# A row sum made with the residual, so that the MLP's centring need not wait for its statistics, and a newly searched order

## The chip, the cores and the metric

One core of a Trainium2 chip runs the whole kernel. The metric is the device time of one execution in microseconds (us); lower is better.

## The reference, cut to what matters

Two layers, each an attention block and an MLP block, on 2048 rows of 512 columns in bf16:

```python
x = x + attention(layernorm(x))       # linear attention, 32 heads, then @ wo
x = x + mlp(layernorm(x))             # relu(gate) * up, then @ W_down
x = x + attention(layernorm(x))
x = x + mlp(layernorm(x))
# layernorm(x) = (x - mean(x)) / sqrt(var(x) + 1e-5), no weights
```

The MLP is homogeneous: a factor on its input comes out squared, as relu(gate) and up both carry it. The kernel feeds it x - mean and multiplies the output by 1/(var + eps).

## The kernel before

The 2048 rows are 16 tiles of 128. Every piece of work is an operation with a cost, a rank ("due") and the buffers it takes. A planner inside the kernel turns them into one emission order; each engine runs its instructions in that order. The ranks (DUE) and the choice of ACT or DVE for copies (PLACE) are tables that a search found beforehand. The hand-over from attention to MLP of tile t:

```python
# attend(l, t, ...)
a = op("PE", mm(4, 512), ..., proj)                       # o @ wo into PSUM
a = op("DVE", dve(512), ..., lambda: nc.vector.tensor_tensor(
    out=x, in0=x, in1=yp.t[:], op=Alu.add), [a], (), [yp], name="resA")
...
# mlp(l, t0, n, ...)
for i in range(n):
    t = t0 + i
    a = stats(l, "B", t, due_x(i), [after[t]])            # bn_stats, bn_aggr -> mean, var
    seen.append(a)
    xc = Buf(p_xn)
    a = op("DVE", CENTRE, due_x(i), lambda t=t, xc=xc: nc.vector.tensor_scalar(
        out=xc.t[:], in0=x_of(t), scalar1=mv[:, t, 0:1], scalar2=None, op0=Alu.subtract), [a], [xc], name="xc", port=2)
    turned.append(turn(xc, ...))                          # transpose; tiles 0 and 1 of a layer on PE, others by DMA
r = op("DVE", ..., tmp = var + EPS, seen); r = op("DVE", ..., rs = 1 / tmp)   # shortened; used by the MLP's residual
...   # gate and up matmuls, relu, product, down matmuls, residual with rs
```

The blocks of the MLP have 1, 1, 2, 4, 4, 2, ... tiles. Only the first one or two must get through attention before PE can start on the MLP at all. For those two hand-overs, one in each layer, the chain "residual, statistics, aggregate, centring, turn, copy" is short of other work.

The softmax here doesn't subtract the row's maximum and nothing guards it: scores larger than these inputs give would overflow.

Of the kernel before, what the change touches and what calls it, by code (L numbers as in the profile page):

```python
# [8 lines left out]
P = 128  # L9
D = 512  # L10
# [26 lines left out]
class Op:  # L37
# [3 lines left out]
    def __init__(self, eng, cost, due, emit, deps=(), takes=(), uses=(), name="", move=0, port=False,  # L41
                 follow=(), alt=None):
        self.eng, (self.occ, self.lat) = eng, cost
        self.due, self.emit, self.name, self.move, self.port = due, emit, name, move, int(port)
        self.deps = [d for d in deps if d is not None]
        self.follow = [d for d in follow if d is not None]
        self.takes, self.uses = list(takes), list(uses)
        self.then, self.behind, self.alt, self.twin = [], [], alt, None
# [162 lines left out]
DVE0 = (85, 170)  # L211
RLN, REXP = ((150, 265), (203, 318)), ((145, 262), (198, 315))
# [13 lines left out]
class K:  # L226
# [9 lines left out]
    "0000000100000001001000000000100000000000010001111000011000011001110000000000011010000001001111001100"  # L236
    "0100000110110100010000011011100101111100101001111000111010100001001101101100100110011001110011001001"
    "1111001110100000000011100010100100000101001110100111000101101010101000101010111001010111100010110100"
    "0"
)  # L240
PHI = dict(POOL=("POOL", "POOL"), DVE=("DVE", "DVE"), BOTH=("DVE", "POOL"))
PHI0 = ["POOL", "POOL", "DVE"] * 5 + ["BOTH"]
PAIRN, PAIRK = 4, T
# [5 lines left out]
    76719491, 69466873, 69464194, 55720479, 42085309, 40348612, 33593703, 42085031, 50665322, 33594228, 56086954,  # L249
    58486545, 100334641, 61163217, 49431745, 41251988, 69056115, 9741064, 80414090, 80414120, 53308772, 80413780,  # L250
    106435297, 49852457, 80414139, 49848882, 56526831, 56526817, 69547873, 53741705, 49852168, 66481170, 68934086,
    55660918, 50246487, 32405931, 57594884, 55662420, 50058741, 44536605, 58281570, 3, 22509044, 49850622, 49848858,
    69548291, 69463783, 49850611, 55051722, 76716792, 0, 55324383, 47430106, 32690380, 59187722, 60929485, 45084743,
    53725584, 55713647, 55727277, 54655971, 49923445, 50246438, 55324400, 55324343, 35442704, 55802924, 35441651,
    55161101, 53685522, 51682019, 33202876, 47809082, 52941970, 53687226, 55701298, 55711066, 55655645, 44505335,
    54950229, 47610086, 55322999, 47811927, 35002194, 55588705, 62960580, 55157588, 53726567, 47768162, 55269518,
    47767416, 55571188, 53304664, 55688755, 55180830, 55625721, 50380932, 40642846, 40645264, 47809620, 55323699,
    57680173, 55268245, 54520833, 53558741, 55098763, 55683455, 55732950, 55683459, 55697315, 55770465, 52825634,
    55713412, 55710946, 55506275, 54950156, 35001190, 54949680, 34999890, 59085355, 62960363, 54948116, 55748897,
    55646532, 56083290, 53268545, 59116845, 55619542, 55763775, 53310977, 55774953, 55764998, 55740543, 52826475,  # L260
    55685321, 52784010, 55711099, 55519531, 56373630, 50382939, 52826205, 52825598, 55778163, 55771090, 55181433,
    55768958, 55684488, 55709355, 55684978, 55522442, 55648291, 55646610, 55689548, 54948629, 55098862, 47766546,
    54948487, 56010726, 55697946, 55693442, 55936025, 53268542, 44506128, 55691384, 55769572, 55545075, 55409199,
    55692897, 55662797, 55667892, 55709660, 55713749, 55700261, 55690361, 55371927, 55946741, 55947245, 55372043,
    55396376, 55760995, 55660101, 55570763, 55708913, 55708943, 50191721, 55658940, 55569634, 55658937, 55655528,
    52824974, 54566163, 55181604, 56093099, 55623488, 55927755, 55388217, 55697886, 55645404, 55667208, 55921043,
    55691484, 55685094, 55623151, 55652318, 55396329, 55703531, 55760168, 55699699, 55388529, 55623507, 55651900,
    55396324, 56045911, 55709610, 55623568, 55048436, 55709159, 56660851, 55240452, 55696214, 55974927, 55693988,
    55741153, 55693228, 55396401, 55665438, 55487833, 55388179, 55703473, 55388150, 55305368, 57292002, 55522439,
    55570606, 54081536, 55694997, 57095763, 45526601, 45175404, 54082167, 55710694, 56661198, 55697150, 54522450,  # L270
    47668141, 45175447, 49709693, 50191138, 48930643, 51185210, 41476757, 41476428, 56663182, 55710691, 55700162,
    55966393, 55623154, 55694078, 55418211, 55667889, 55662695, 50622534, 54522884, 55759099, 54522768, 55305365,
    53814510, 54207260, 51926549, 56731158, 22533505, 86923532, 49054124, 54577294, 50454445, 56663443, 26743223,
    64933030, 26742771, 41476589, 77848357, 55701636, 46564931, 86922882, 76909815, 56851302, 56665549, 49600025,
    49129654, 50619771, 50620709, 50622827, 56301309, 54209613, 56114277, 54821759, 49333488, 51487502, 52263956,
    39762113, 19221682, 41476432, 41476507, 40958443, 51486441, 50279390, 16984712, 37300570, 50960427, 49597502,
    35848215, 39760598, 24648533, 41476504, 55699989, 55704953, 48137801, 50278843, 46562185, 37300567, 49597307,
    49597499, 35844120, 55705982, 39761347, 49335617, 38759704, 49337568, 39761346, 55750849, 56154495, 33592791,
    56153063, 32405860, 51221336, 55803472, 55693594, 55803225, 55321390, 55802697, 53688156, 49597175, 49597541,
    49597913, 49596963, 58672801, 49543902, 49597043, 49596659, 55778023, 55771093, 55123240, 55776845, 55771414,  # L280
    55772175, 53557771, 53310277, 53304643, 44505573, 53310550, 55124938, 56045945, 55661057, 55711116, 55624256,
    55667825, 55396537, 56736587, 57094903, 54082104, 57408271, 54209459, 57094884, 55827685, 46563699, 56440267,
    55828521, 55702687, 46562936, 55705068, 48140907, 48140902, 56553271, 55701218, 55705063, 55720810, 56440270,
    48141651, 55702429, 55696714, 55697995, 59129153, 55703718, 55704014, 55827014, 48137480, 46562610, 30585230,
    58655341, 49560287, 21530914, 52917937, 47182136, 30584484, 55701037, 46563696, 52917833, 41444195, 41443940,
    47181589, 47181495, 41443844, 55700488, 53497782, 38496984, 56130655, 55690360, 55704606, 53137802, 55693769,
    55703325, 53137820, 55692042, 50947124, 55405040, 50987789, 41443966, 41414378, 55870566, 52917866, 55300343,
    55700485, 52129878, 61996903, 62505784, 55697736, 53137801, 55550154, 55700626, 55740601, 55699572, 55699299,
    55704914, 55699024, 58344346, 62506293, 50451565, 49470778, 53245447, 53278134, 49336219, 55704076, 55886670,
    55697360, 53497785, 55550159, 55699902, 55700360, 55698793, 55698582, 52841760, 55869605, 55108122, 54090734,  # L290
    55300268, 62506063, 62660753, 62506806, 55705573, 49344780, 55886105, 55700933, 49470866, 56146496, 55700624,
    55692773, 55692770, 55701615, 55740476, 49312541, 55752952, 49765942, 55886212, 55430767, 55238713, 55977103,
    55691820, 55688056, 47612654, 55699803, 55700555, 55697628, 55700835, 55741749, 55700975, 55702709, 55575076,
    55692884, 53991858, 53991972, 53990466, 54779534, 53853809, 54779664, 55691422, 55704463, 55620232, 55701498,
    55691964, 55738452, 55702685, 56001882, 55694740, 55702008, 55709199, 55691466, 55067255, 54761274, 56123195,
    55807312, 53991318, 53863952, 53762021, 55604349, 55704395, 55702362, 55614451, 55885531, 55702411, 55692752,
    55709972, 55702819, 56002178, 55480865, 55231139, 54147794, 57042018, 52613586, 55611316, 55693850, 55704710,
    55704869, 55540072, 55704035, 55707614, 55708907, 55702786, 55415742, 55707642, 55704187, 55610312, 55706936,
# [146 lines left out]
def kernel(  # L445
# [328 lines left out]
    def attend(l, t, due, eq, made, how):  # L774
# [4 lines left out]
        for k in range(3):  # L779
# [36 lines left out]
            for b in range(NB)], [a] + l_wo, [yp], [oT], name="proj")  # L816
        x = x_of(t)
        a = op("DVE", dve(512), due + 3, lambda: nc.vector.tensor_tensor(out=x, in0=x, in1=yp.t[:], op=Alu.add), [a],  # L818
               (), [yp], name="resA")
        return pe, a  # L820


# [207 lines left out]
```

## Time and profile before

| | before |
|---|---|
| time, median of 6 runs | 386.45 us (385.96 to 386.70) |
| span of the profiled run | 384.4 us |
| PE busy, DVE, ACT | 375.9, 316.6, 211.1 us |
| matmuls, of which fillers (warm-up included) | 2834, 15 |

In the views, one line is a group of instructions: start, length, engine, source line, operation, output<-inputs, shapes, count; in brackets the engine's idle time just before and who ended it. PE is the matmul engine, PEld its weight loads. Of the names, xn is a centred tile and xnTB its turned (transposed) form, o is the attention's output and oT the same turned, N holds copied numerators of the attention. Fillers are matmuls on zeros, whose result nobody reads.

Busy PE hides refills, and the trace of the changed kernel lacks the records of 45 of its matmuls, so busy and idle sums of these two traces cannot be compared (a later trace of it has all 2832; see the end). I use an **account of lost PE time** instead. All 2832 or 2834 weight loads are in the traces, one per matmul, in program order. Each matmul is given its streaming time, columns/2.4 + 2.5 ns; the traces show that rate in unbroken streams (4 matmuls of 512 columns 0.86 us, 16 of 128 columns 0.89 us). Fillers (matmuls on zeros, whose result nobody reads) count nothing. The work is then 365.98 us. What the clock shows at a weight load, less the work done by then, is the time lost so far. The work mark (12 us of work, 48 us of work, ...) is the same point of progress only roughly, since orders differ, and weight loads start ahead of their matmul (in before by 0.05 to 0.21 us in a stream, by up to 0.74 where the matmul waits). So differences below 0.2 us between marks say little.

### The profile page before, as it was taken

To read this page: it belongs to the slowest core of one execution; us is meant where nothing else is said; L and a number is where in the kernel's file an instruction comes from. 1 tells how busy PE (TensorE), PEld (TensorE's weight loads), DVE (VectorE), ACT (ScalarE), POOL (GpSimd) and SP (SyncE) were. 2 spreads that over 40 slices of the span, in tenths; PEclk is the share of its full clock that TensorE was granted. 3 is DMA by queue.
4 is the path that set the end of the run, shared out by engine and by line. 5 is a ranking of instruction groups with operands and counts; after the bars stand their busy time and mean duration, and the time that the engine had idled before them with its cause. 6 is when DMAs were issued, how large, how long until landed. Compare 5 with 4: busy or idle time off the path is not lost.

```text
span 384.4 us, 7669 instructions
## 1 busy us (share of the span) xinstructions
PE 375.9 (98%) x2834; PEld 226.1 (59%) x2834; DVE 316.6 (82%) x804; ACT 211.1 (55%) x545; POOL 40.6 (11%) x43
## 2 busy tenths in 40 slices
PE   8999998999999999999999999999999999999996
PEld 5454555877654445445666654587765445446775
DVE  6999999999999999586686688999999795565442
ACT  5999999634557215573274479955444513421431
POOL 0256720000002100050031021000000000000000
PEclk9999999999999999999999999999999999999999
DMA  8398730133222224201110000012333313002110
GB/s 226 78 232 219 176 118 2 38 69 63 41 57 55 44 41 57 55 2 34 29 35 2 15 15 1 2 32 47 79 67 81 72 23 88 0 14 77 32 31 29
DMA packets 60869, 22.83 MB, mean 59 GB/s; under 512 B 52672, under 2 KB 59808, under 8 KB 60832
## 3 DMA queue, kind: packets, MB, share of 16 engines
q1 hardware_dynamic: 60416, 21.95, 25.3%
q10 hardware_dynamic: 416, 0.39, 0.4%
q8 instruction: 22, 0.36, 0.4%
q14 instruction: 15, 0.12, 0.1%
HBM read 7.91 MB, written 2.10 MB: 26 GB/s over the span
## 4 chain that ended last, share of the span: by engine, by line
PE 84%; DVE 12%; issue 2%; ACT 1%; DVEq 0%
PE b L878 33%; PE b L911 17%; PE b L676 7%; PE b L682 7%; PE b L814 5%; PE b L764 5%; PE q L782 3%; PE b L854 3%; PE q L723 2%; DVE bstB L637 1%; DVE hT L886 1%; PE q L584 1%; DVE bstA L637 1%; DVE pr L807 1%; DVE gu L591 1%
## 5 line engine op out<-in xcount | busy, mean ns | idle before, releaser
L878 PE MATMUL b<-xnTB,wgu 128*128 128x128 bf16 (+2 forms) x1200 | 151.8, 279 | 0.3 <-ACT xnTB L590 0.3
L878 PEld LDWEIGHTS <-wgu 128*128 128x128 bf16 x1200 | 98.0, 98 | 44.1 <-issue 0.4
L911 PE MATMUL b<-wd,hT 128*128 128x512 bf16 (+2 forms) x363 | 85.9, 373 | 0.0
L882 ACT ACTIVATE gu<-b 128x512 bf16<-128x512 f32 (+1 forms) x83 | 48.4, 584 | 57.9 <-PE b L878 54.3
L706 POOL TENSOR_TENSOR phiK<-ek,sk 128x512 bf16<-128x512 bf16 x37 | 39.9, 1101 | 193.2 <-ACT sk L697 190.7
L886 DVE TENSOR_TENSOR hT<-gu 128x512 bf16<-128x512 bf16 (+1 forms) x83 | 34.8, 420 | 24.2 <-ACT gu L590 22.9
L911 PEld LDWEIGHTS <-hT 128*128 128x128 bf16 (+1 forms) x363 | 34.0, 98 | 30.8 <-DVE hT L886 0.3
L679 ACT ACTIVATE ek<-b 128x512 bf16<-128x512 f32 x64 | 35.4, 604 | 16.6 <-PE b L676 16.5
L687 DVE TENSOR_REDUCE sk<-ek 128x64 f32<-128x1024 bf16 x32 | 38.5, 1211 | 3.4 <-ACT ek L679 3.2
L768 ACT ACTIVATE Eq<-b 128x512 bf16<-128x512 f32 x64 | 36.1, 623 | 1.6 <-PE b L764 1.4
L814 PE MATMUL b<-wo,oT 128*128 128x512 bf16 x128 | 32.9, 379 | 0.5 <-ACT oT L590 0.5
L918 DVE SCALAR_TENSOR_TENSOR X<-b,rsB,X 128x512 bf16<-128x512 f32 (+1 forms) x33 | 23.6, 724 | 11.8 <-PE b L911 11.6
L590 ACT CAST gu<-b 128x512 bf16<-128x512 f32 (+1 forms) x42 | 24.4, 581 | 16.2 <-PE b L878 16.1
L590 ACT CAST N<-q 128x384 bf16<-128x384 f32 (+1 forms) x60 | 26.9, 464 | 11.3 <-PE q L782 8.5
L682 PE MATMUL b<-wv,xnTA 128*128 128x512 bf16 x128 | 32.5, 379 | 0.2 <-DVE xnTA L591 0.2
L676 PE MATMUL b<-Wk,xnTA 128*128 128x512 bf16 x128 | 32.4, 379 | 0.1
L591 DVE CAST gu<-b 128x512 bf16<-128x512 f32 (+1 forms) x41 | 26.4, 646 | 6.7 <-PE b L878 6.5
L764 PE MATMUL b<-xnTA,Wq 128*128 128x512 bf16 x128 | 31.7, 379 | 0.0
L782 PE MATMUL q<-R,Eq 128*128 128x144 bf16 x256 | 28.2, 226 | 0.7 <-DVE R L745 0.6
L782 PEld LDWEIGHTS <-Eq 128*128 128x128 bf16 x256 | 20.6, 98 | 12.8 <-issue 1.4
L818 DVE TENSOR_TENSOR X<-X,b 128x512 bf16<-128x512 bf16 x32 | 21.6, 676 | 4.2 <-PE b L814 3.9
L637 DVE BATCH_NORM_STATS2 bstA<-X 128x6 f32<-128x512 bf16 x32 | 21.3, 679 | 1.5 <-DMA X<-in_A_x_dram 1.3
(72 smaller groups left out, 390.7 us busy)
## 6 DMA issues: line engine op xcount, KB each, us to landing
out_dram<-X SPq DMA_DIRECT2D x15, 128.0 KB, 1.7
X<-in_A_x_dram SPq DMA_DIRECT2D x6, 256.0 KB, 3.3
wgu<-in_B_W_gate_dram SPq DMA_DIRECT2D x4, 344.0 KB, 3.7
wgu<-in_B_W_up_dram SPq DMA_DIRECT2D x4, 344.0 KB, 4.1
wd<-in_B_W_down_dram SPq DMA_DIRECT2D x5, 256.0 KB, 3.4
wv<-in_A_wqkv_dram SPq DMA_DIRECT2D x2, 256.0 KB, 4.3
wo<-in_A_wo_dram SPq DMA_DIRECT2D x4, 128.0 KB, 3.0
oT<-o SPq DMA_TRANSPOSE x28, 2.4
```

The costliest lines, as they stand in the source:

```text
L590: both = {"ACT": ("ACT", act(cols), lambda: nc.scalar.copy(out=out_(), in_=in_()), False), "DVE": ("DVE", dve(cols), lambda: nc.vector.ten ...
L676: k = op("PE", mm(4, 512), due, lambda: [nc.tensor.matmul(kp.t[:], lhsT=xnTA[c][:, b, cols], rhs=Wk2[:, b, :], start=(b == 0), stop=(b == ...
L682: v = op("PE", mm(4, 512), due_v, lambda: [nc.tensor.matmul(vp.t[:], lhsT=xnTA[c][:, b, cols], rhs=wv[:, b, :], start=(b == 0), stop=(b == ...
L687: a = op("DVE", SUM16, due, lambda: nc.vector.tensor_reduce(out=sk.t[:, row, :], in_=ek.t[:].rearrange("p g s (h f) -> p (g s h) f", f=DH) ...
L706: e.tensor_tensor(out=ph.t[:].rearrange("p g s (h f) -> p (g s h) f", f=DH)[:, lo:lo + n], in0=ek.t[:].rearrange("p g s (h f) -> p (g s h) ...
L764: q = op("PE", mm(4, 512), due(c, b), lambda b=b, qp=qp: [nc.tensor.matmul(qp.t[:], lhsT=Wq2[:, m, b * P:(b + 1) * P], rhs=xnTA[c][:, m, : ...
L782: pe.append(op("PE", mm(len(groups), GE), due, lambda ps=ps, groups=groups: [nc.tensor.matmul(ps.t[:, n * GE:(n + 1) * GE], lhsT=Eq[c][:, ...
L814: a = op("PE", mm(4, 512), due + 3, lambda: [nc.tensor.matmul(yp.t[:], lhsT=oT.t[:, b, :], rhs=wo[:, b, :], start=(b == 0), stop=(b == NB ...
L878: nc.tensor.matmul(ps.t[:, q * W:(q + 1) * W], lhsT=wgu[:, s, b, g * P:(g + 1) * P], rhs=xT.t[:, b, 0:W], start=(b == 0), stop=(b == NB - 1))
L882: nc.scalar.activation(out=gu.t[:, 0, 0:cols], in_=gp.t[:, 0:cols], func=AF.Relu)
L886: nc.vector.tensor_tensor(out=h.t[:, f0 * W:f0 * W + cols], in0=gu.t[:, 0, 0:cols], in1=gu.t[:, 1, 0:cols], op=Alu.mult)
L911: nc.tensor.matmul(yp.t[:, 0:c1 - c0], lhsT=h.t[:m, f * W + i * P:f * W + (i + 1) * P], rhs=wd[:m, f, c0:c1], start=(f == 0), stop=(f == N ...
```

## The change

Tiles 0 and 1 of each layer take the row sum together with the residual, and centre with it at once: xc = 512 x - sum(x). The statistics still run, later; the factor 512 is taken out of 1/(var + eps) as 512 squared. With it comes a new set of tables, so the order of nearly every instruction changed. The diff, cut to its core (switches SPLIT and SUM_ON_PE stay off and change nothing):

```diff
+RESSUM = (750, 850)
+SUM_ON_PE, SPLIT, SUMMED = False, False, 2
 PLACE = ( ...301 new bits... )
 DUE = ( ...2105 new ranks... )
+    rowsum = new("rowsum", [2, 2], F32)
         x = x_of(t)
-        a = op("DVE", dve(512), ..., nc.vector.tensor_tensor(out=x, in0=x, in1=yp.t[:], op=Alu.add), ..., name="resA")
+        if t < SUMMED:
+            a = op("DVE", RESSUM, ..., nc.vector.scalar_tensor_tensor(
+                out=x, in0=yp.t[:], scalar=1.0, in1=x, op0=Alu.mult, op1=Alu.add,
+                accum_out=rowsum[:, l, t:t + 1]), ..., name="resS")
+        else: ...as before
-            a = op("DVE", CENTRE, ..., tensor_scalar(scalar1=mv[:, t, 0:1], op0=Alu.subtract), [a], [xc], name="xc")
+            if t < SUMMED:
+                a = op("DVE", CENTRE, ..., tensor_scalar(scalar1=float(D), scalar2=rowsum[:, l, t:t + 1],
+                    op0=Alu.mult, op1=Alu.subtract), [after[t]], [xc], name="xc")
+            else: ...as before
-   ve: scalar1=EPS, scalar2=None, op0=Alu.add
+   ve: scalar1=EPS, scalar2=float(D * D) if t0 < SUMMED else 1.0, op0=Alu.add, op1=Alu.mult
```

## The prediction

> **What bounds the kernel now.** I read the page first: busy shares, then the 40 slices, then the groups.
>
> ```profile
> PE 375.9 (98%) x2834; PEld 226.1 (59%) x2834; DVE 316.6 (82%) x804; ACT 211.1 (55%) x545; POOL 40.6 (11%) x43
> ...
> PE   8999998999999999999999999999999999999996
> ...
> PEclk9999999999999999999999999999999999999999
> ```
>
> TensorE (PE) works for 375.9 of the span's 384.4 us at the full clock; no other engine comes near. So the room is what PE does not use, 8.5 us. The windows view splits it (columns: stretch, its length, then busy us of PE, weight loads, DVE, ACT, POOL).
>
> ```profile
> 0.00:1.26 1.26, 0.00 (x0) 0.00 (x1) 0.44 (x6) 0.00 (x0) 0.66 (x6) 1.00 0.00 0
> 1.26:16.00 14.74, 14.02 (x97) 8.20 (x98) 12.57 (x35) 11.01 (x27) 0.05 (x1) 1.00 0.68 180
> ...
> 55.00:59.00 4.00, 3.74 (x29) 2.07 (x27) 3.36 (x12) 3.73 (x13) 0.00 (x0) 1.00 0.00 0
> 59.00:66.00 7.00, 5.36 (x53) 3.28 (x52) 6.69 (x22) 6.95 (x22) 0.00 (x0) 1.00 0.00 0
> ...
> 138.00:180.00 42.00, 41.52 (x253) 21.05 (x251) 35.25 (x80) 21.02 (x54) 5.31 (x5) 1.00 0.23 39
> ...
> 238.00:249.00 11.00, 10.08 (x79) 5.90 (x78) 10.06 (x33) 10.63 (x33) 0.00 (x0) 1.00 0.01 1
> ...
> 381.30:384.40 3.10, 0.00 (x0) 0.00 (x0) 0.57 (x2) 0.00 (x0) 0.00 (x0) 1.00 0.27 85
> ```
>
> Start 1.26 and end 3.10 belong to setup and to the last store. The other 4.1 us are gaps: 0.72 while the inputs load, 0.26 at 55 us (building R), 1.64 in 59 to 66 us, 0.48 in 138 to 180, 0.92 in 238 to 249. The change aims at the two places where attention hands the first tile to the MLP, at 62 to 66 us and 246 to 249 us. PE's timeline there (start, length, what; in brackets the idle time before and who ended it):
>
> ```profile
> 63.61 1.04 PE L814 MATMUL b<-wo,oT 128*128 128x512 bf16 x4 [0.29 <-ACT oT L590]
> 64.56 0.40 PE L628 MATMUL b<-ident,xn 128*128 128x128 bf16 x4
> 64.80 0.54 PE L782 MATMUL q<-R,Eq 128*128 128x144 bf16 x6
> 65.63 1.05 PE L878 MATMUL b<-xnTB,wgu 128*128 128x128 bf16 x16 [0.30 <-ACT xnTB L590]
> ...
> 248.18 0.40 PE L628 MATMUL b<-ident,xn 128*128 128x128 bf16 x4 [0.56 <-DVE xn L833]
> ```
>
> And DVE's at the first of them:
>
> ```profile
> 62.49 0.68 DVE L818 TENSOR_TENSOR X<-X,b 128x512 bf16<-128x512 bf16 x1
> 63.21 0.69 DVE L637 BATCH_NORM_STATS2 bstB<-X 128x6 f32<-128x512 bf16 x1
> 63.94 0.18 DVE L638 BATCH_NORM_AGGREGATE mvB<-bstB 128x2 f32<-128x6 f32 x1
> ...
> 64.15 0.35 DVE L833 TENSOR_SCALAR xn<-X,mvB 128x512 bf16<-128x512 bf16 x1
> ```
>
> The chain is residual, statistics, aggregate, centring, turn on PE, copy, first gate matmul. From the start of the residual to the start of centring it is 64.15 - 62.49 = 1.66 us in layer 0. In layer 1 the same two instructions start at 245.88 and 247.78: 1.90 us. The page's chain that ended last has its bstB share at 1%, so the change can touch little of the end.
>
> **What the Trainium skill says.** (1) Perfetto Trace Analysis, "Identifying the Most-Contended Engine", warns that matmul busy share is a bad measure of closeness to roofline because matmuls are pipelined. The trace agrees: 16 gate matmuls after a wait take 1.05 us, 0.89 us in the chain of waits where none precedes them, so "busy" hides 0.16 us per gap. I use it as a surcharge. (2) TensorE: Matmul & The Clock Gate, "Single matmul latency", gives about 166 ns warm on top of streaming, which is that 0.16. (3) VectorE: DVE Perf Modes, "Why PSUM operands drop a tier", caps an fp32 PSUM operand at one element per cycle. So the new residual form loses no faster mode: the addition from PSUM has a mean of 676 ns today, the addition of two bf16 SBUF tensors of the same width (o) 408 ns. (4) The same page, "Two Vector instructions with no wait between them", says an instruction that also writes its accumulator is two, the main one and an accumulator read. Nothing in this trace shows one; I count an extra small instruction.
>
> **The change, part by part.**
>
> Residual, tiles 0 and 1 of each layer (4 instructions): a tensor_tensor of 676 ns becomes a scalar_tensor_tensor from PSUM with a row sum. The same form without sum exists as the MLP's residual (L918): 740 ns mean at 512 columns. For the accumulator read I estimate 60 to 170 ns, from the one-column instructions of this trace (59 ns for a one-element memset, 170 ns for the aggregate). Together 0.85 us, 0.17 more each, 4 x 0.17 = 0.7 us more DVE work.
>
> Centring, 4 instructions: x*512 minus the row sum in place of x minus the mean; same form, 0.35 us, no saving. It waits for the residual alone. The factor 512 is undone in "ve", which takes eps and 512 squared in one instruction instead of eps alone: no added instruction.
>
> Statistics and aggregates stay, all 64 of the MLP and attention norms; four pairs leave the chain and only have to be ready for the MLP's residual, whose first instruction starts at 83.9 us. That slack is many us.
>
> So the chain from residual start to centring goes from 1.66 to about 0.85 + 0.1 hand-over = 0.95 us in layer 0 (0.7 earlier) and from 1.90 to 0.95 in layer 1 if nothing lies between (0.95 earlier). PE can gain only its own wait. Ceiling: (0.30 + 0.16) + (0.56 + 0.18, since the turn took 0.40 instead of its 0.22) = 1.20 us.
>
> Below the ceiling: in layer 0 centring would be done near 62.49 + 0.95 + 0.35 = 63.8 us, just after PE began tile 1's projection at 63.61, which holds PE to 64.47. The turn started at 64.56 anyway. So either it stays put and gains 0.1, or it is put ahead of the projection, PE waits 0.2 there and saves 0.46 later. I take 0.25. In layer 1 the turn could start about 247.15, fill a slot before PE runs dry at 247.62, but the copy from PSUM (0.67) then ends near 248.1, and the next projection's operand, copied 247.55 to 248.21, is no earlier. PE would be dry from about 247.84 (0.22 of turn moved ahead) to 248.15 instead of 0.56: a gain of 0.25. Sum 0.5 us. Tile 1's xn is not waited for: PE had work when it arrived at 68.0 us, so those two of the four gain nothing.
>
> The rest of the diff is a new order for the whole kernel: every due value and the placement of copies between ACT and DVE. PE's work is the same. Of the 4.1 us of gaps, 3.2 lie outside the two waits above; each of some 14 carries its 0.16 too, and PE runs seven filler matmuls (15 in all, 8 of them warm-up; 0.22 each, 1.5 us) while the start waits. That pool is about 3.2 + 12 x 0.16 + 1.5 = 6.6 us. A new search that takes a sixth of it gives 1.1 us. This is a judgement, not a reading. Total 0.5 + 1.1 = 1.6 us.
>
> **Rivals.**
>
> (a) The wait is replaced by another, so that the direct gain is nil: PE waits for o, oT or the copy of the turned tile. For it: in 59 to 66 us PE waited six times for such links (0.57, 0.25, 0.23, 0.29, 0.30 and smaller), ACT is busy 6.95 of 7.00 us there and DVE 6.69. Against: the layer 1 gap names xn itself. It makes 386 to 386.5 with a neutral order.
>
> (b) DVE becomes the bound: +0.7 us in stretches where it is full. Against: only two of the four longer residuals lie on the chain, and DVE has 18% free over the span. The statistics pushed back could delay tile 2's chain; that costs 0.2 to 0.5 us: 386.5 to 387.
>
> (c) The new order collects more of the gaps than I say, say half of 6.6 us plus the 1.2 ceiling: 4.5 us, 382.2. Against: the kernel was already searched, and the start is held by transfers.
>
> (d) The new order fits the chip worse than its plan: PE in-order stalls of 1 to 2 us, 387 to 388.5.
>
> **Range and chances.** From 386.69: minus 1.6 is 385.1 us. The three timed runs spread 0.57. Rival (a) with a small gain of order reaches about 386.5, half of (c) reaches 383.4; the range is 383.4 to 386.7. Two per cent is 7.7 us, below 379.0. The gaps inside are 4.1, their surcharge about 2.2, fillers 1.5: 7.8 us, so faster needs practically all of it at once: 0.01. Slower, above 394.4, would need twice the present gaps again: 0.01. Same: 0.98.
>
> **What would show it.** Right: new residual instructions of 0.80 to 0.90 us; centring starts within 1.0 us of their start; statistics after it; no PE wait named xn over 0.3 us at the second layer's hand-over; PE busy within 1.5 us of 375.9 and PE idle between 6 and 8 us. If the gain lies mostly outside 59 to 66 and 238 to 249 us, the order made it and not the row sum. Wrong: a residual over 1.1 us, a centring that still starts 1.6 us after, or PE gaps in those stretches as large under another name (rival a); DVE waits growing on the next tiles (b); gain beyond 4 us (c).

## The result, and the profile after

The changed kernel takes 383.87 us (median of 6 runs, 383.81 to 383.96), before 386.45; the ratio is 0.9935, 95% interval 0.9922 to 0.9947. Ratios here are the mean time of one kernel's fast runs over the mean of the other's of the same rounds, so not quite the ratio of the medians. By the rule of 2% that is "same", and it is 2.6 us faster, clear of the noise.

The first hand-over on DVE in the changed kernel:

```profile
61.41 0.68 DVE L997 SCALAR_TENSOR_TENSOR X<-b,X 128x512 bf16<-128x512 f32 x1
62.02 0.08 DVE L997 DVE_READ_ACCUMULATOR X<-b,X 128x1 f32 x1
62.13 0.35 DVE L1018 TENSOR_SCALAR xn<-X,rowsum 128x512 bf16<-128x512 bf16 x1
62.40 0.69 DVE L810 BATCH_NORM_STATS2 bstB<-X 128x6 f32<-128x512 bf16 x1
63.12 0.18 DVE L811 BATCH_NORM_AGGREGATE mvB<-bstB 128x2 f32<-128x6 f32 x1
```

Reading out the row sum is an instruction of its own, as the Trainium skill has it (VectorE: DVE Perf Modes, "Two Vector instructions with no wait between them"), and it takes 0.08 us, of which 0.07 lie inside the residual's own 0.68. Centring starts 0.72 us after the residual; it was 1.66. PE at the two hand-overs (the first four lines the first):

```profile
62.54 0.40 PE L797 MATMUL b<-ident,xn 128*128 128x128 bf16 x4 [0.22 <-DVE xn L1018]
62.80 1.04 PE L992 MATMUL b<-wo,oT 128*128 128x512 bf16 x4
63.67 0.35 PE L955 MATMUL q<-R,Eq 128*128 128x144 bf16 x3
63.86 1.95 PE L1068 MATMUL b<-xnTB,wgu 128*128 128x128 bf16 x32
...
246.11 0.39 PE L797 MATMUL b<-ident,xn 128*128 128x128 bf16 x4
246.33 1.03 PE L992 MATMUL b<-wo,oT 128*128 128x512 bf16 x4
247.19 0.35 PE L955 MATMUL q<-R,Eq 128*128 128x144 bf16 x3
247.38 1.06 PE L1068 MATMUL b<-xnTB,wgu 128*128 128x128 bf16 x16
```

The turn of the centred tile goes ahead of the second tile's projection, at the price of a wait of 0.22 us, and the first gate matmul follows with no wait. In the second layer the turn, the projection and the gate matmuls stand without a gap; before, PE stood 0.56 us for xn there. The new order also has a gap that before has not:

```profile
104.59 1.48 PE L1044 MATMUL b<-wgu,xnTB 128*128 128x192 bf16 x16
107.14 0.29 PE L955 MATMUL q<-R,Eq 128*128 128x144 bf16 x2 [1.06 <-DVE N L753]
```

The account of lost PE time, for all kernels (us lost between two marks of work done; the names are explained below, the last column is the loss up to 300 us of work):

```
kernel                                   0-48  48-60  60-126  126-222  222-240  240-300   to 300
                                       start  hand-over 1               hand-over 2
before                                   8.85   2.76   0.08     1.47     1.09     0.38     14.63
after                                    7.73   2.46   1.11     0.49     0.60    -0.14     12.25
after again (first time)                 8.10   2.45   1.09     0.49     0.61    -0.14     12.60
after again (second time)                7.85   2.45   1.28     0.59     0.59    -0.14     12.62
e1 new order, old chain                  7.68   3.36   1.09     0.55     1.55    -0.14     14.09
e2 old order, row sum                    9.18   2.69   0.08     1.45     1.48     0.39     15.27
e3 old order, sum made, not used         8.84   2.77   0.09     1.45     1.10     0.38     14.63
e4 new start, old rest                   7.79   2.76   0.09     1.45     1.10     0.47     13.66
e5 new to 216 us, old rest               8.20   2.46   1.09     0.50     1.10     0.44     13.79
e6 old to 212 us, new rest               8.63   2.76   0.08     1.68     0.61    -0.14     13.62
e7 new order, mended                     7.71   2.45   0.35     0.55     0.60    -0.14     11.52
e8 new order, sum for tile 0 alone       7.82   2.45   1.15     0.49     0.77    -0.14     12.54
e9 new first 8 us, old rest              8.96   2.77   0.08     1.46     1.09     0.39     14.75
e10 mended, again                        8.02   2.46   0.35     0.50     0.59    -0.14     11.78
```

After the start the columns repeat within 0.1 us for the same instructions, mostly (0.2 once). The start differs by up to 0.5 from run to run, with the same instructions (8.63 to 9.18 for the old one, mean 8.88 of 4; 7.68 to 8.20 for the new one, mean 7.89 of 8; e4 and e9 mix the two); what makes it differ was not traced. The zero of that column is a matter of choice, by 0.2 us, the same for all. From before to after, 2.38 us went: start 1.12, first hand-over 0.30, second 0.49, 126 to 222 us 0.98, end 0.52, and 1.03 us were lost anew at 60 to 126.

### The profile page after: what moved, and what is told of

It is laid out like the page before. It is cut to its first block, busy times and chain, and to the rows that moved or that the text cites. A ratio compares the mean times of both kernels' runs of the same rounds, so it can differ in the third digit from the quotient of the medians.

```text
span 382.0 us, 7622 instructions
## 1 busy us (share of the span) xinstructions
PE 371.5 (97%) x2787; PEld 224.4 (59%) x2832; DVE 311.1 (81%) x798; ACT 215.0 (56%) x554; POOL 41.9 (11%) x44
## 4 chain that ended last, share of the span: by engine, by line
PE 77%; DVE 17%; DMA 2%; issue 2%; ACT 1%; DVEq 0%
PE b L1068 31%; PE b L1101 17%; PE b L855 5%; PE b L849 5%; PE b L992 5%; PE b L937 5%; PE q L955 3%; PE b L1044 2%; PE q L896 2%; DMA xnTA<-xn 2%; DVE pr L980 1%; DVE bstA L810 1%; DVE bstB L810 1%; DVE sk L860 1%; DVE N L753 1%
## 5 line engine op out<-in xcount | busy, mean ns | idle before, releaser
L1101 PE MATMUL b<-wd,hT 128*128 128x512 bf16 (+3 forms) x349 | 82.3, 372 | 0.7
L879 POOL TENSOR_TENSOR phiK<-ek,sk 128x512 bf16<-128x512 bf16 x38 | 41.2, 1102 | 192.3 <-ACT sk L870 164.1
L1076 DVE TENSOR_TENSOR hT<-gu 128x512 bf16<-128x512 bf16 (+1 forms) x83 | 34.0, 414 | 15.4 <-ACT gu L752 14.2
L752 ACT CAST gu<-b 128x512 bf16<-128x512 f32 (+1 forms) x50 | 28.4, 570 | 24.0 <-PE b L1068 20.4
L941 ACT ACTIVATE Eq<-b 128x512 bf16<-128x512 f32 x64 | 37.3, 629 | 3.3 <-PE b L937 3.1
L752 ACT CAST N<-q 128x384 bf16<-128x384 f32 (+1 forms) x59 | 26.1, 464 | 12.4 <-PE q L955 6.7
L849 PE MATMUL b<-Wk,xnTA 128*128 128x512 bf16 x123 | 31.6, 379 | 0.4 <-DVE xnTA L753 0.2
L992 PE MATMUL b<-wo,oT 128*128 128x512 bf16 x120 | 31.3, 379 | 0.4
L753 DVE CAST gu<-b 128x512 bf16<-128x512 f32 (+1 forms) x33 | 21.8, 665 | 11.1 <-PE b L1068 11.1
L980 DVE TENSOR_TENSOR pr<-N,w 128x1024 bf16<-128x1024 bf16 x32 | 21.8, 683 | 0.7
```

Of the source, the lines that this page charges most:

```text
L752: both = {"ACT": ("ACT", act(cols), lambda: nc.scalar.copy(out=out_(), in_=in_()), False), "DVE": ("DVE", dve(cols), lambda: nc.vector.ten ...
L849: k = op("PE", mm(4, 512), due, lambda: [nc.tensor.matmul(kp.t[:], lhsT=xnTA[c][:, b, cols], rhs=Wk2[:, b, :], start=(b == 0), stop=(b == ...
L879: e.tensor_tensor(out=ph.t[:].rearrange("p g s (h f) -> p (g s h) f", f=DH)[:, lo:lo + n], in0=ek.t[:].rearrange("p g s (h f) -> p (g s h) ...
L941: done.append(op("ACT", act(512), due(c, b), lambda b=b, s=s, qp=qp: nc.scalar.activation(out=Eq[c][:, b, s, :], in_=qp.t[:], func=AF.Exp, ...
L992: a = op("PE", mm(4, 512), due + 3, lambda: [nc.tensor.matmul(yp.t[:], lhsT=oT.t[:, b, :], rhs=wo[:, b, :], start=(b == 0), stop=(b == NB ...
L1101: nc.tensor.matmul(yp.t[:, 0:c1 - c0], lhsT=h.t[:m, f * W + i * P:f * W + (i + 1) * P], rhs=wd[:m, f, c0:c1], start=(f == 0), stop=(f == N ...
```

## The experiments

The question is what made the 2.6 us: the row sum, or the new order that came with it. The planner cannot answer it: with the new tables and the old chain it stops with the message that no instruction can go. So I wrote out what the planner made, order, engine and buffer of each operation, as plain lists. The written-out forms of both kernels have the same instructions on every engine as the originals. In the experiments only the named instructions are moved or changed. All twelve runs gave correct results, and those of one call ran on one chip beside before (in the second call, with e4, e6, e8 and the changed kernel again, that is the nine runs of before from the first call and one more on the same chip).

**e1: the new order with the old chain.** For tiles 0 and 1 of both layers:

```diff
-RES, CEN = ((0, 0), (0, 1), (1, 0), (1, 1)), ((0, 0), (0, 1), (1, 0), (1, 1))
+RES, CEN = (), ()                       # old residual, old centring
 order:  residual ...
-        xc, ..., stats, ..., aggr
+        stats, aggr, xc
```

> The changed kernel's emission order kept instruction by instruction, but with the old residual (no row sum) and the old centring (reads the mean); the two statistics instructions stand in front of the centring again for tiles 0 and 1 of both layers. Nothing else moves. Theory 'sum': the hand-overs gained because centring no longer waits for the statistics, so this order must now wait for them there, about 0.7 us at each first tile, 1.0 to 1.5 us in all: 384.9 to 385.4. Rival 'order': the new order alone made the 2.6 us, the sum is decoration: 383.7 to 384.2. Before is 386.45, after 383.87.

Measured: 385.85 us, ratio to before 0.9994 (0.9981 to 1.0007). All but 0.2 us of the gain is gone. PE waits just where the sum had served:

```profile
63.43 0.40 PE L592 MATMUL b<-ident,xn 128*128 128x128 bf16 x4 [1.16 <-DVE lnB L822]
...
247.83 0.40 PE L592 MATMUL b<-ident,xn 128*128 128x128 bf16 x4 [0.67 <-DVE xn L817]
```

(The first is put down to lnB; xn ends at 63.37, beside it, and is what the turn reads.) The account has 0.90 us more at the first hand-over (3.36 for 2.46) and 0.95 at the second (1.55 for 0.60), the rest unchanged. So the rival "the order alone" fell: in this order the sum is worth 1.85 us. It went further than my range, which stopped at 385.4. But the new order's gains outside the hand-overs are all still there in e1; it comes out level with before because at the hand-overs this order without the sum is 1.06 us worse than the old one (3.36 for 2.76 and 1.55 for 1.09). An order that is new elsewhere and old at the hand-overs, without the sum, was not built. So 1.85 us is what the sum is worth in this order, and not shown to be what any kernel without it must lose.

**e2: the old order with the row sum.**

```diff
-RES, CEN = (), ()
+RES, CEN = ALL, ALL                     # tiles 0 and 1 of both layers
 order:  residual ...
-        stats, aggr, xc
+        xc, stats, aggr
```

> The old kernel's order kept, but with residual and row sum in one instruction for tiles 0 and 1 of both layers and the centring put in front of its statistics on DVE; every other engine's order is the old one. Theory 'sum': the PE waits of 0.30 and 0.56 us named xnTB copy and xn shrink, 0.4 to 0.8 us gained: 385.6 to 386.1. Rival 'order': without a new order the next wait (o, oT, the copy of the turned tile) takes its place: 386.3 to 386.7.

Measured: 386.62 us, ratio 1.0016 (1.0004 to 1.0029): slower, not faster. The first hand-over gained 0.07 us and the second lost 0.39; another 0.33 stands in the start, where nothing was changed, and is within what the start differs by. PE at the second hand-over in e2, with one copy on DVE:

```profile
247.70 0.39 PE L592 MATMUL b<-ident,xn 128*128 128x128 bf16 x4
248.50 1.04 PE L787 MATMUL b<-wo,oT 128*128 128x512 bf16 x4 [0.41 <-ACT oT L547]
249.38 0.29 PE L750 MATMUL q<-R,Eq 128*128 128x144 bf16 x2
249.74 1.44 PE L863 MATMUL b<-xnTB,wgu 128*128 128x128 bf16 x23
...
252.24 0.42 DVE L548 CAST N<-q 128x256 bf16<-128x256 f32 x1
252.71 0.35 PE L750 MATMUL q<-R,Eq 128*128 128x144 bf16 x3
```

and in before:

```profile
248.41 1.03 PE L814 MATMUL b<-wo,oT 128*128 128x512 bf16 x4
249.28 0.29 PE L782 MATMUL q<-R,Eq 128*128 128x144 bf16 x2
249.40 0.78 PE L878 MATMUL b<-xnTB,wgu 128*128 128x128 bf16 x11
...
251.58 0.42 DVE L591 CAST N<-q 128x256 bf16<-128x256 f32 x1
252.08 0.35 PE L782 MATMUL q<-R,Eq 128*128 128x144 bf16 x3
```

Everything in e2 is 0.24 us late here, from what it lost before (the first tile's residual starts at 246.12 for 245.88). The turn moved up by 0.48 us (247.70 for 248.18), 0.72 against the residual, but the projection behind it waits for oT, the second tile's turned output, and gains only 0.15 against it. The gate matmuls come 0.10 later against it, as the copy of the turned tile stands behind the statistic and seven small instructions on DVE (249.01 in e2, 248.64 in before). The wait changed its name; that is the first rival of my prediction, as it stood there. The larger part of the 0.39, some 0.29 us, is lost after that: the second tile's centring now also stands in front of its statistic, the copy N behind them comes late (252.24 for 251.58), and PE waits for it (252.71 for 252.08). I read this from the two traces; I did not build the old order with the sum for the first tile alone.

**e3: the sum made but not used, old order.** Only the residual instruction differs from before.

```diff
-RES, CEN = (), ()
+RES, CEN = ALL, ()
```

> The old kernel's order with only the residual changed: it also makes the row sum, which nobody reads; centring still takes the mean. It measures the cost of the new instruction alone. My prediction's term: 0.17 us each, at least one on the chain per layer: 386.7 to 386.9. Against it, the trace of the changed kernel (0.68 us plus an accumulator read of 0.08 that overlaps its end, against 0.68 for the old one): 386.4 to 386.6, no difference beyond 0.1 us.

Measured: 386.24 us beside 386.07, ratio 1.0003 (0.9990 to 1.0016), and the account's columns are those of before within 0.02 from 48 us on. The new instruction costs nothing that can be seen.

**e4 and e9: the start.** The new order and placement for what was planned to start in the first 20 us (e4) or 8 us (e9), then the old order with the old chain.

```diff
 order:
-old
+new[planned start < 20 us]  +  old[without those]       # e9: 8 us
 RES, CEN = (), ()
```

> The changed kernel's order and placement for every instruction planned to start in the first 20 us, then the old kernel's order, with the old residual and centring. By the account of lost PE time the new order's start is worth 1.2 us (8.1 lost before the first 12 us of work are done, 6.9 in the changed kernel): 385.0 to 385.5. If the start's gain is given back later (the old rest can't use it, being held by ACT and DVE up to 66 us), 386.0 to 386.6.

> As the kernel with the new start, but the new order and placement cover only what was planned to start in the first 8 us (who copies the turned key weights, ACT or DVE, and in which order). In the old kernel's trace DVE waits 0.38 us for one of those copies at 7.3 us and the second tile's normalisation starts at 10.79, in the changed kernel's at 10.14. If those copies are the start's gain: about 0.6 us, 385.4 to 385.9 beside a before of about 386.2. If the gain is made between 8 and 20 us: 386.0 to 386.5.

Measured: e4 385.27 us, ratio 0.9978 (0.9964 to 0.9992), 0.9 below before; e9 386.67 beside 386.45, ratio 1.0006 (0.9993 to 1.0019). So the start's gain is real without any row sum, and it is made by what was planned between 8 and 20 us. Part of DVE's timeline in e9:

```profile
8.76 0.17 DVE L606 BATCH_NORM_AGGREGATE mvA<-bstA 128x2 f32<-128x6 f32 x1
9.32 0.69 DVE L548 CAST Wq<-b 128x512 bf16<-128x512 f32 x1 [0.39 <-PE b L570]
9.93 0.17 DVE L606 BATCH_NORM_AGGREGATE mvA<-bstA 128x2 f32<-128x6 f32 x1
```

and in e4:

```profile
8.85 0.16 DVE L606 BATCH_NORM_AGGREGATE mvA<-bstA 128x2 f32<-128x6 f32 x1
8.93 0.66 DVE L605 BATCH_NORM_STATS2 bstA<-X 128x6 f32<-128x512 bf16 x1
9.51 0.16 DVE L606 BATCH_NORM_AGGREGATE mvA<-bstA 128x2 f32<-128x6 f32 x1
```

In e9, as in before, DVE takes a copy of the folded query weights between two tiles' norms (in e9 it also waits 0.39 us for PE there, in before it does not); in e4 ACT takes it and the next tiles' statistics come at once. The key matmuls of the next tiles start at 14.38 us in e4 and at 15.40 in e9. That this copy is the cause is argued from the two traces; I did not move it alone.

**e5 and e6: two halves.** e6 is the old order up to 212 us with the old chain in layer 0, then the new order with the row sum in layer 1. e5 is the complement, new up to 216 us with the sum in layer 0, then the old.

```diff
-one order throughout
+e6: old[planned start < 212 us] + new[the others],  RES, CEN = layer 1's tiles
+e5: new[planned start < 216 us] + old[the others],  RES, CEN = layer 0's tiles
```

> The other half: the old order up to 212 us with the old forms in layer 0, then the changed kernel's order with the row sum in layer 1. It holds the second hand-over and the end. The account of lost PE time gives 0.5 for the hand-over and 0.5 after it: 385.2 to 385.7. If the hand-over's gain needs something prepared earlier than 212 us, or the seam costs as much: 386.0 to 386.6.

> The changed kernel's order up to 216 us with the row sum in layer 0 only, then the old order with the old forms in layer 1: the complement of the kernel that kept the old order up to 212 us. If the gains of the parts add up, this one has what that one lacked, 2.4 minus 1.0 less the seam: 384.6 to 385.2. If they don't add (each half needs the other), 385.5 or more.

Measured: e6 385.13 us, ratio 0.9974 (0.9960 to 0.9988), just below its expected 385.2 to 385.7; e5 385.26, ratio 0.9967 (0.9954 to 0.9979), just above its expected 384.6 to 385.2. The shares add up: 0.26% and 0.33% make 0.59%, and the changed kernel has 0.57 to 0.68%. So the second layer's hand-over with the end, and all that lies before, are two nearly equal parts that do not need each other.

**e8: the row sum for the first tile of each layer alone**, new order; tile 1 has the old chain, as in e1.

```diff
-RES, CEN = ALL, ALL
+RES, CEN = ((0, 0), (1, 0)), ((0, 0), (1, 0))
```

> The changed kernel's order with the row sum for the first tile of each layer alone; the second tile has the old residual, its statistics in front of its centring. My prediction's step 'tile 1's centred tile is not waited for' says no difference: 383.7 to 384.1. If the second tile's chain is on the path as well, it costs up to 0.7 us per layer: 384.4 to 385.2.

> The changed kernel once more, unaltered, so that the runs of this call have it beside them on the same chip: 383.7 to 384.0, ratio 0.993 to 0.995.

Measured: e8 384.10 us, ratio 0.9949 (0.9936 to 0.9961); the changed kernel 383.78, ratio 0.9943 (0.9929 to 0.9956). The intervals overlap. The account has 0.16 more at the second hand-over and nothing at the first, about as little as it can tell; the medians differ by 0.32. So tile 1's sum is worth 0.2 to 0.3 us at most, within the noise.

**e7 and e10: the new gap mended.** What DVE and POOL did in the changed kernel before its 1.06 us gap:

```profile
102.66 0.98 DVE L973 TENSOR_TENSOR m<-m 128x32 f32<-128x32 f32 x1
103.56 0.68 DVE L879 TENSOR_TENSOR phiK<-ek,sk 128x512 bf16<-128x512 bf16 x1
...
102.53 1.06 POOL L879 TENSOR_TENSOR phiK<-ek,sk 128x512 bf16<-128x512 bf16 x1 [0.41 <-ACT sk L870]
```

The sum of 32 columns takes 0.19 us elsewhere and 0.98 here, to the end of POOL's product. The Trainium skill names a reason, and this trace agrees with it: SBUF — State Buffer, "Who interferes with whom", says that a DVE instruction with two SBUF inputs and a GpSimd one that reads SBUF exclude each other, and whoever comes second waits. The edit puts that sum earlier, and fills POOL's time with instructions that this rule lets pass:

```diff
 DVE order, 100.5 to 105 us:
-m, sk, ve, resA, den, phi, rden, stats, r2, w, phi, pr
+m, den, sk, ve, resA, rden, stats, r2, phi, w, phi, pr
```

> The changed kernel with four DVE instructions moved near 101 to 104 us: the small sum 'den' in front of the statistic sk, and rden, one row statistic and one reciprocal in front of the phi product. In the changed kernel's trace one 'm' instruction there takes 0.98 us instead of 0.19, from just after a POOL product starts to its end, DVE is late and PE then waits 1.06 us for an N copy. Theory 'shared': DVE's two-input product or sum waits while POOL's runs; with work there that doesn't wait, the gap goes: 382.8 to 383.2. Rival: DVE is late for its amount of work, the gap stays: 383.7 to 384.0.

> The changed kernel unaltered, beside the mended one of this call: 383.7 to 384.1.

> The mended kernel again, so that it and the changed one stand on the same chip: 382.9 to 383.3, 0.6 to 0.9 us below the changed one.

Measured: 383.08 us, ratio 0.9920 (0.9907 to 0.9934). Again: 383.15 (383.01 to 383.34) beside the changed kernel's 383.89 (383.67 to 384.22) on the same chip; ratios to before 0.9915 and 0.9932. No run of the one is as slow as any of the other. In e7's trace:

```profile
100.76 0.19 DVE L768 TENSOR_TENSOR m<-m 128x32 f32<-128x32 f32 x1
...
102.67 0.34 DVE L770 RECIPROCAL m<-m 128x32 f32<-128x32 f32 x1
102.93 0.63 DVE L605 BATCH_NORM_STATS2 bstB<-X 128x6 f32<-128x512 bf16 x1
...
106.38 0.28 PE L750 MATMUL q<-R,Eq 128*128 128x144 bf16 x2 [0.33 <-DVE N L548]
```

The reciprocal and the statistics ran at their usual length while POOL worked from 102.74 to 103.79. PE's gap fell from 1.06 to 0.33 us, the account's column from 1.11 to 0.35. The same work in DVE's queue, only in another order, removed it. So this version beats both kernels by moving four instructions.

## Why the prediction was right or wrong, point by point

**What bounds the kernel: right. The size of the whole: low.** 2.6 us came, 1.6 were named, and 383.87 lies in the range, near its low end. The gain stayed far from 2%. That the range reached so low owes something to a slip: it was put down to "half of (c)", but half of 4.5 us from 386.69 gives 384.4; 383.4 is what half of the 6.6 us alone gives.

**The cost of the new residual: mis-sized.** The step said 0.85 us each, 0.17 more than before. It measured 0.679 with 0.082 for the accumulator read, nearly all of it under the residual's end; e3 found no cost. The first layer's centring starts 0.72 after the residual and not 0.95, the second layer's 1.05 after (244.56 to 245.61), as DVE puts two PSUM copies in between.

**What the hand-overs gain: the total about right, in part by luck.** I said 0.25 at each, at most 1.20 together, from the waits PE had. The account shows 0.30 and 0.49, under that ceiling. But my working let the sum gain this with the neighbours nearly as they were, and in the old order it gained nothing (e2). The step that fell short is "PE can gain only its own wait": it asks what the sum is worth in the order as it stands. In the new order it is worth 0.90 and 0.95 (e1), as that order is arranged around it and is worth less than the old one at these places when it is missing. The gain came from both together; my sum of two separate terms, 0.5 and 1.1, has no place for that.

**Rival (a), the wait renamed: shown, but for the fixed order only.** In e2 oT and the copy of the turned tile took over, the two that the prediction's working for layer 1 had named, and then the copy N. In layer 0 its alternative "put ahead of the projection, PE waits 0.2" is what the new order does: the wait is 0.22.

**Tile 1's sum gains nothing: nearly.** e8 puts it at 0.2 to 0.3 us at most, within the noise; in the old order it seems to cost 0.29 (e2).

**The new order's share: right in kind, low in size.** I judged 1.1 us. Start 1.1, end 0.5 and middle about zero (0.98 gained, 1.03 lost anew) make 1.6. e4 shows the start without the sum; the split of e6's gain into hand-over and end rests on the account alone.

**Rival (b), DVE as the bound: not seen** in the changed kernel in the form that I gave it; the late copy N in e2 is of that kind. DVE did become late at 103 us, not from more work but from POOL's product. **Rivals (c) and (d)** each happened in part: the order collected more than I said, and once fitted the chip worse than its plan.

**My own tests.** "No PE wait named xn over 0.3 us" held. PE's busy and idle sums, which I had also named, can be read from the second trace of the changed kernel, which has all 2832 matmuls: busy 374.4 us, 1.6 below before, and idle 8.0, both a hair outside what I had named. Of the 2.0 us by which its span is shorter, 1.6 came out of "busy", though the work differs by two fillers alone: these sums were a bad sign. And "if the gain lies mostly outside the two stretches, the order made it and not the row sum" was a bad test: of 2.38 us, 1.59 lie outside, and these are still there in e1, but without the sum this order gives 1.06 us of them back at the hand-overs.

What stays open: which of the start's instructions makes its 1.0 us, what the old order lost at 126 to 222 us that the new one does not, and how much of the 2.6 us an order searched for the old chain could reach.

## What to carry to other kernels

Shortening a chain in front of the busiest engine and reordering the work around the shorter chain are one change: here neither the chain alone (+0.16%) nor this whole order without it (-0.06%) gained, together they gave -0.6%. That does not make every part of the order useless alone: its first 20 us gave -0.22% without the sum (e4). To find what each is worth, freeze the emitted order and swap one piece at a time, and read the loss against the work done by then, not against busy time. Look at each new gap of a searched order: one here came from DVE meeting POOL, and moving four instructions gave another 0.2%.

## What the Trainium skill lacked or had wrong

- VectorE: DVE Perf Modes, "Two Vector instructions with no wait between them", has the accumulator read as an instruction of its own, but no page that I read gives its time: 80 to 83 ns here, starting 0.61 us into a residual of 0.68, and no cost in e3.
- TensorE: Matmul & The Clock Gate, "Back-to-back issue gap", puts a sustained stream of weight load and matmul pairs at some 81 ns for 128 columns and 131 ns for 512. The runs show 1.79 us for 32 matmuls of 128 columns (56 ns) and 0.86 us for 4 of 512 (216 ns): the page's own isolated formula fits the streams too.
